# Down projection of a gated feed-forward layer: one token tile's second product moved to the end and split in two column pieces

## Chip, cores, metric

The kernel runs on one core of a Trainium2 chip. The metric is device time of one execution in microseconds (us), lower is better. The median before was 273.38 us (3 runs, 273.16 to 274.22). Five things work side by side on the core: the tensor engine (PE; PEld is its weight loading), the vector engine (DVE), the scalar engine (ACT), GpSimd (POOL), and the queues that start DMAs (here mostly SP's). Data lies in the on-chip memory SBUF; PE writes its sums to PSUM, used here as eight banks.

## The reference

```python
def reference(x, w_gate, w_up, w_down):          # x 32x32x1024, F = 3584, all bf16
    return (_gelu(x @ w_gate) * (x @ w_up)) @ w_down
```

So there are 1024 tokens; the last step, the down projection, multiplies a 1024x3584 matrix by a 3584x1024 one. The change touches only this step.

## The kernel before

The down projection is one level of a Strassen scheme: the operands are seen as 2x2 blocks, and seven block products are made in the order 1, 2, 7, 5, 6, 3, 4. Products 1 and 2 multiply the bf16 data directly; the operands of the others are held as f32r (fp32r in the profile), for 7, 5 and 6 sums or differences made by DVE. Each product is 4 token tiles of 128 rows times 14 steps of 128 (NK = 14), each step a matmul of 512 columns. A PSUM bank holds one tile. Product 1 is used twice: product 2 is added to it to give an output block (the sum goes out from `o11`), and a copy of it in the banks PB is where product 6 is added.

```python
        PA, PB = (0, 1, 2, 3), (4, 5, 6, 7)
        F, H = 0.2266, 0.216                      # planned us of one matmul, f32r and bf16
        begin = {}
        now = base
        for n in (1, 2, 7, 5, 6, 3, 4):
            begin[n] = now
            now += 4 * NK * (H if n < 3 else F)
        end = now
        EDGE = 4

        def sweep(n, banks, start, stat, mov, done, prep=None):
            steps = [(t, k) for k in range(EDGE) for t in range(3)] + [(3, k) for k in range(EDGE)]
            steps += [(t, k) for k in range(EDGE, NK - EDGE) for t in range(4)]
            steps += [(t, k) for t in range(4) for k in range(NK - EDGE, NK)]
            if n < 3:
                steps = [(t, k) for t in range(4) for k in range(NK)]
            # ... [cut: for every step one matmul; after a tile's last step, done(t, planned time)]

        sweep(1, PA, True, lambda k, t: ht(0, 0, k, t), lambda k: wd[0][0][:, k, :],
              lambda t, at: act(bank(PB[t]), bank(PA[t]), COPY, at))

        def done2(t, at):
            act(o11[:, t, :], bank(PA[t]), COPY, at)
            out_dma(0, t, 0, o11[:, t, :])
        sweep(2, PA, False, lambda k, t: ht(0, 1, k, t), lambda k: wd[1][0][:, k, :], done2)
        # ... [cut: prep7, prep5, prep6, prep3, prep4: DVE and ACT make the operands of the other products]
        def done4(t, at):
            if t % 2 == 0:
                pr.add("dve", "tensor_copy", late[:, 2, t, :], bank(PA[t]), at=at)
            else:
                act(late[:, 2, t, :], bank(PA[t]), COPY, at)
            out_dma(1, t, 0, late[:, 2, t, :])
        # ... [cut: sweeps 7, 5, 6, 3]
        sweep(4, PA, False, lambda k, t: S[:, c_at(1, k), t * P:(t + 1) * P], one_w(2), done4, prep4)
```

Every instruction goes through a small recorder that finds the dependences itself, in SBUF by cells of 256 bytes and in PSUM by whole banks. And on every engine but PE the instructions are put in the order of a planned time `at`, so the order is fixed before the kernel runs.

```python
    GRAIN = 256
    def cells(self, ap):
        # ... [cut]
        found.update(range(s // self.GRAIN, (s + run - 1) // self.GRAIN + 1))
    def finish(self, nc, es):
        for e in self.ENGINES:
            if e != "pe":
                self.ops[e].sort(key=lambda op: (op.at, op.index))
```

## Time and profile before

| quantity | value | from |
|---|---|---|
| time, median of 3 runs | 273.38 us | timed runs |
| span of the profiled execution | 976.1 us | the page |
| start of one 512-column matmul to the next | 0.84 us | timeline |
| ACT copy of 128x512 / DVE copy of 128x512 | 0.597 / 0.692 us | instruction groups by shape |
| store of 128 KB, issue to landing | 1.7 us | DMA issues |
| end of the last matmul to the end of the span | 2.76 us | trace: 976.13 - 973.37 |

The page of the kernel before, its head, its chain that ended last and the costliest group (columns of a group: busy us, mean ns of one, then idle time before):

```profile
span 976.1 us, 3280 instructions
PE 966.8 (99%) x1182; PEld 436.0 (45%) x1192; DVE 208.5 (21%) x237; ACT 134.8 (14%) x210; POOL 36.6 (4%) x23
...
PE 99%; issue 1%; ACT 0%
...
L117 PE MATMUL ps<-S,T 128*128 128x512 f32 x560 | 465.4, 1102 | 0.0
```

PE bounds the kernel. But this execution is 3.6 times as long as the timed ones: matmuls started 0.84 us apart. Its records give a granted clock of 1.00 all the same, so what slowed it is not shown. The end of its timeline (columns: start us, length us, engine, instruction, count, idle time before and its releaser):

```profile
959.09 14.28 PE L117 MATMUL ps<-T,S 128*128 128x512 f32 x17
...
966.84 0.60 ACT L117 ACTIVATE arena<-ps 128x512 bf16<-128x512 f32 x1 [12.01 <-PE ps L117]
...
973.40 0.60 ACT L117 ACTIVATE arena<-ps 128x512 bf16<-128x512 f32 x1 [5.97 <-PE ps L117]
```

17 matmuls in 14.28 us are 0.84 us each. The last thing PE releases is an ACT copy of 0.60 us; then only the store of 128 KB remains.

### The profile page before, as it was taken

Reading aid. Unit: us, or ns where it says so; the run is one execution under the profiler, and the core shown is the slowest. Engines: PE = TensorE matmul, PEld = TensorE weight load, DVE = VectorE, ACT = ScalarE, POOL = GpSimd, SP = SyncE. Lnnn points to the kernel's source line nnn. Section 1 sums busy time; section 2 is a strip of 40 time slices with the busy share of each in tenths; the row PEclk is TensorE's granted clock in tenths of the full one; section 3 lists DMA queues with packets and bytes.
Section 4 is the critical chain, followed back from the end, with each engine's and each line's share of the span. In section 5 each row is a group of like instructions: output and inputs, shape, how many; then the busy total and the mean of one; then the engine's idle time right before and its main releaser. Section 6 shows DMA issues by size and latency. Waiting matters only on the chain.

```text
span 976.1 us, 3280 instructions
## 1 busy us (share of the span) xinstructions
PE 966.8 (99%) x1182; PEld 436.0 (45%) x1192; DVE 208.5 (21%) x237; ACT 134.8 (14%) x210; POOL 36.6 (4%) x23
## 2 busy tenths in 40 slices
PE   9999999999999999999999999999999999999998
PEld 3222235555555555555444443442224555555554
DVE  0112222123212321231120202045000433114100
ACT  0011122111221112121111120100000000012110
POOL 0000000000000000001101010000000000000000
DMA  5530100101301003003000020400000000000000
GB/s 129 134 82 0 43 0 1 43 0 37 92 1 43 0 0 119 0 2 85 1 0 0 2 74 0 150 1 1 0 11 11 1 0 0 0 0 22 16 5 21
DMA packets 46895, 27.46 MB, mean 28 GB/s; under 512 B 8480, under 2 KB 46880, under 8 KB 46880
## 3 DMA queue, kind: packets, MB, share of 16 engines
q1 hardware_dynamic: 44656, 25.30, 9.4%
q10 hardware_dynamic: 2224, 1.97, 0.8%
q8 instruction: 9, 0.15, 0.1%
q14 instruction: 6, 0.05, 0.0%
HBM read 23.33 MB, written 2.10 MB: 26 GB/s over the span
## 4 chain that ended last, share of the span: by engine, by line
PE 99%; issue 1%; ACT 0%
PE ps L117 99%; ACT arena L117 0%
## 5 line engine op out<-in xcount | busy, mean ns | idle before, releaser
L117 PE MATMUL ps<-S,T 128*128 128x512 f32 x560 | 465.4, 1102 | 0.0
L117 PEld LDWEIGHTS ps<-S,T 128*128 128x128 f32 x560 | 240.2, 429 | 221.0 <-issue 212.7
L117 PE MATMUL ps<-T,S 128*128 128x512 f32 x224 | 185.2, 1098 | 0.0
L117 PE MATMUL ps<-arena 128*128 128x512 bf16 x186 | 155.2, 1105 | 3.4 <-issue 3.4
L117 PEld LDWEIGHTS ps<-T,S 128*128 128x128 f32 x224 | 96.0, 429 | 88.1 <-issue 88.1
L117 PEld LDWEIGHTS ps<-arena 128*128 128x128 bf16 x192 | 41.4, 221 | 113.9 <-issue 108.7
L117 PE MATMUL ps<-arena,hT 128*128 128x512 bf16 x109 | 90.2, 1106 | 1.9 <-issue 1.9
L117 ACT ACTIVATE tmp<-ps 128x512 f32<-128x512 f32 x64 | 38.1, 597 | 335.3 <-PE ps L117 335.3
L117 DVE TENSOR_TENSOR hT<-tmp,ps 128x512 bf16<-128x512 f32 x56 | 38.5, 687 | 189.9 <-PE ps L117 187.5
L117 DVE TENSOR_TENSOR tmp<-ps,tmp 128x512 f32<-128x512 f32 x28 | 19.4, 692 | 244.4 <-PE ps L117 244.4
L117 ACT ACTIVATE ps<-ps 128x512 f32<-128x512 f32 x44 | 25.6, 582 | 233.7 <-PE ps L117 233.7
L117 DVE TENSOR_TENSOR T<-arena,T 128x1024 fp32r<-128x1024 bf16 x42 | 51.0, 1220 | 29.9 <-PE ps L117 29.8
L117 POOL TENSOR_TENSOR T<-arena 128x1024 fp32r<-128x1024 bf16 x17 | 35.9, 2123 | 528.4 <-DVE T L117 499.5
L117 PEld LDWEIGHTS ps<-arena,hT 128*128 128x128 bf16 x112 | 24.5, 221 | 67.1 <-issue 66.5
L117 DVE TENSOR_TENSOR T<-arena 128x1024 fp32r<-128x1024 bf16 x25 | 30.0, 1219 | 104.6 <-PE ps L117 104.6
L117 PE MATMUL ps<-S 128*128 128x512 f32 x56 | 46.3, 1092 | 0.0
L117 PEld LDWEIGHTS ps<-S 128*128 128x128 f32 x56 | 23.9, 427 | 22.0 <-issue 22.0
L117 DVE TENSOR_TENSOR ps<-ps,tmp 128x512 f32<-128x512 f32 x32 | 22.3, 698 | 53.0 <-PE ps L117 53.0
L117 ACT ACTIVATE tmp<-tmp 128x512 f32<-128x512 f32 x28 | 17.7, 631 | 67.7 <-DVE tmp L117 67.7
L117 PE MATMUL ps<-arena,tmp 128*128 128x512 bf16 x31 | 26.1, 1100 | 0.5 <-issue 0.5
L117 ACT ACTIVATE hT<-ps 128x512 f32<-128x512 f32 x14 | 8.4, 597 | 67.8 <-PE ps L117 67.8
L117 DVE TENSOR_TENSOR S<-hT,S 128x1024 fp32r<-128x1024 bf16 x7 | 8.6, 1226 | 39.0 <-PE ps L117 39.0
(29 smaller groups left out, 112.6 us busy)
## 6 DMA issues: line engine op xcount, KB each, us to landing
arena<-in_w_down_dram SPq DMA_DIRECT2D x4, 1792.0 KB, 9.4
arena<-in_w_gate_dram SPq DMA_DIRECT2D x10, 512.0 KB, 4.1
arena<-in_w_up_dram SPq DMA_DIRECT2D x10, 512.0 KB, 5.4
out_dram<-arena SPq DMA_DIRECT2D x12, 128.0 KB, 1.7
arena<-in_w_gate_dram SPq DMA_DIRECT2D x4, 256.0 KB, 5.0
arena<-in_w_up_dram SPq DMA_DIRECT2D x4, 256.0 KB, 5.0
arena<-in_w_up_dram ACTq DMA_DIRECT2D x4, 128.0 KB, 4.7
arena<-in_w_gate_dram ACTq DMA_DIRECT2D x2, 256.0 KB, 2.8
```

What stands on the lines that cost most here:

```text
L117: ins = name(eng, *args, **kw) if callable(name) else getattr(eng, name)(*args, **kw)
```

## The change

Intent: what follows the last matmul (copy, issue, store) is paid in full, so let the last piece of work be small. One tile of product 2 waits until everything else is done. It is split at column 384, into two banks; the first piece is copied by ACT and stored while PE still works on the second. As product 1's copy in PB is used up by product 6, tile 3 of product 1 is kept in an SBUF tile `p1` meanwhile. A sweep begins with three of its tiles and holds the fourth back for a while, so that ACT has time to empty that tile's bank; which tile is held back changes in product 7. The diff, cut to its core:

```diff
+        p1 = sb("p1", [P, 512], FP32)
         for n in (1, 2, 7, 5, 6, 3, 4):
             begin[n] = now
-            now += 4 * NK * (H if n < 3 else F)
-        end = now
+            now += (3 if n == 2 else 4) * NK * (H if n < 3 else F)
+        end = now + NK * H
 # ... [cut] in sweep: product 7 holds back tile 2, the others tile 3; product 2 has 3 tiles
+            held = 2 if n == 7 else 3
+            steps = [(t, k) for k in range(EDGE) for t in range(4) if t != held] + [(held, k) for k in range(EDGE)]
             if n < 3:
-                steps = [(t, k) for t in range(4) for k in range(NK)]
+                steps = [(t, k) for t in range(5 - n) for k in range(NK)]
 # ... [cut]
+        def done1(t, at):
+            act(bank(PB[t]), bank(PA[t]), COPY, at)
+            if t == 3:
+                act(p1[:, :], bank(PA[t]), COPY, at)
 # ... [cut] after sweep 4:
+        pieces = ((PB[0], 0, 384), (PB[1], 384, 512))
+        for b, c0, c1 in pieces:
+            act(ps[:, b, 0:c1 - c0], p1[:, c0:c1], COPY, begin[4] + 6)
+        for b, c0, c1 in pieces:
+            for k in range(NK):
+                mm(b, ht(0, 1, k, 3), wd[1][0][:, k, c0:c1], False, k == NK - 1, add=True)
+            if c0 == 0:
+                act(o11[:, 3, c0:c1], ps[:, b, 0:c1 - c0], COPY, end)
+            else:
+                pr.add("dve", "tensor_copy", o11[:, 3, c0:c1], ps[:, b, 0:c1 - c0], at=end)
+            dma("sp", out_r[:, 3, c0:c1], o11[:, 3, c0:c1], end, "out")
```

## The prediction

> **What bounds the kernel now.** The tensor engine: the page gives PE busy for 99% of the span, DVE 21%, ACT 14%, and 99.0% of the chain that ended last is matmuls. The profiled execution took 976.1 us though the timed runs took 273.38: its matmuls start every 0.84 us (17 in 14.28 us, timeline of the end), while 1182 matmuls in 273 us leave at most 0.23 us each. Its "granted clock 1.00" can't be right. The Trainium skill, "TensorE: Matmul & The Clock Gate", Part 1, warns that clock events are unreliable and that the gate has been seen stuck at one quarter; 0.84 us agrees with that (its warm 215.7 ns for 512 columns, times 3.9). So I use the profile for ACT, DVE and DMA durations and for order, not for PE durations or waits.
>
> **What the change does.** The fourth token tile's second product (14 matmuls of 512 columns, bf16) leaves the second sweep and comes last, as 14 of 384 and 14 of 128 columns. Added: one ACT copy of the first product to SBUF, and two back into free PSUM banks (0.60, then an estimated 0.48 and 0.25 us, from 0.597 us for 128x512), where ACT is mostly idle: off the path. The later sweeps begin 14 x 0.216 = 3.02 us (the program's own slot length) earlier. DVE prepares their operands at 1.22 us a piece. By the program's schedule the seventh product's are ready 5.6 us before it begins, 2.6 after the change. For the fifth and sixth, the earlier PE also frees their slots earlier, so DVE's waits move along. The tile held back in the seventh product becomes the third, whose bank is now released last: 12 matmuls still cover the 0.6 us copy. I expect no new PE stall.
>
> **Cost on the path: PE.** The columns are the same, but 14 more weight loads and matmuls come. With the skill page's warm rate (N/2.4 + 2.5 ns), 14 x 162.5 + 14 x 55.8 = 3.06 us against 3.02; at the page's sustained 81 ns per 128-column matmul, 3.41. The slow trace has 128-column transposes every 0.21 us, a quarter of 0.84, so there the load hides. Cost 0.04 to 0.4 us, estimate 0.2.
>
> **Gain on the path: the tail.** Before, the last matmul's end (973.38) is followed by a 0.60 us ACT copy, a 0.33 us DMA issue and the landing (1.7 us); the span ends at 976.1: 2.7 us. After, a DVE copy of 128x128 ends it, estimated at 0.29 us (128x512 took 0.692, 128x256 of bf16 0.292). The 384-column copy runs on ACT during the last 14 matmuls. The last DMA carries 32 KB instead of 128, in 256-byte rows; its time is mostly fixed: 0 to 0.2 us. Gain 0.3 to 0.5 us.
>
> **Net.** 0.1 to 0.3 us faster, on 273.38, whose own runs spread over 1.06. Predicted 273.15 us, 272.4 to 273.9. Faster by over 2%: 0.01; within 2%: 0.98; slower by over 2%: 0.01.
>
> **What would show the steps.** 1196 matmuls; no gap at the starts of the seventh, fifth, sixth product; a DVE copy of about 0.29 us after the last matmul instead of 0.60 on ACT; landing of the last DMA 1.5 to 1.7 us; last matmul to span end about 2.3 instead of 2.7 us; the last 28 matmuls within 3.5 us at full clock (four times that at a quarter).
>
> **What would make it wrong.** A DVE-bound stretch at full clock, hidden in the slow profile, so that the earlier sweeps meet unready operands (up to +3 us); slow small stores; weight loads that 128-column matmuls don't hide (over 0.4 us).

## The result, and the profile after

273.11 us median (272.7 to 273.49, 6 runs) against 273.44 for the kernel before in the same rounds (273.04 to 274.22, 6 runs). Ratio 0.9985, 95% interval 0.9968 to 1.0003. A ratio here is the mean time of one kernel's fast runs over that of the other's of the same rounds, so it isn't quite the ratio of the medians quoted. The change is the same as before by the 2% measure, inside the predicted 272.4 to 273.9.

The profile after was taken at full clock. To have something to lay it beside, the kernel before was run once more as an experiment (run 1 below), and its profile is at full clock too. Head and end of the chain (start us, length us, what), kernel before at full clock:

```profile
span 271.0 us, 3290 instructions
PE 267.2 (99%) x1192; PEld 190.4 (70%) x1192; DVE 203.2 (75%) x237; ACT 131.9 (49%) x210; POOL 37.1 (14%) x23
...
268.27 0.02 issue
268.29 0.60 ACT arena L117
```

After the change:

```profile
span 271.2 us, 3314 instructions
PE 267.6 (99%) x1197; PEld 191.8 (71%) x1206; DVE 203.5 (75%) x238; ACT 132.8 (49%) x213; POOL 37.2 (14%) x23
...
269.01 0.02 issue
269.04 0.29 DVE o L117
```

DVE is really 75% busy, not 21%. The last link of the chain went from 0.60 us on ACT to 0.29 us on DVE. (1206 matmuls are in the program after and 1192 before, by the weight loads; some PE records are missing.) The spans alone, 271.0 and 271.2, would say that the change cost 0.2 us. They can't be compared like that: the code ahead of the down projection is the same in both, yet the down projection's first bf16 weight load starts at different times. Weight loads around that point, before and after:

```profile
180.41 1.62 PEld L117 LDWEIGHTS ps<-arena,hT 128*128 128x128 bf16 x9 [0.26 <-issue]
```

```profile
181.12 0.98 PEld L117 LDWEIGHTS ps<-arena,hT 128*128 128x128 bf16 x6 [0.26 <-issue]
```

That is 0.70 us apart. Over 13 profiles it lies between 180.41 and 181.47 us, a scatter of 1.06 us that comes from the part that nobody changed. So I measure from this weight load ("the anchor") to the end of the span, and split that at the end of the last matmul (which the profile models; the sum doesn't depend on it):

| us | before (run 1) | after |
|---|---|---|
| anchor to end of last matmul | 87.84 | 87.88 |
| end of last matmul to end of span ("tail") | 2.76 | 2.20 |
| anchor to end of span | 90.60 | 90.09 |

The change takes 0.52 us off: +0.04 on PE, -0.56 in the tail (worked out before rounding, here and below, so a last digit can differ by one). The tail in the two timelines. Before, at full clock:

```profile
267.87 0.39 PE L117 MATMUL ps<-T,S 128*128 128x512 f32 x1
268.11 1.14 SPq L117 DMA_DIRECT2D out_dram<-arena  x2
268.29 0.60 ACT L117 ACTIVATE arena<-ps 128x512 bf16<-128x512 f32 x1 [1.22 <-PE ps L117]
```

After (PE's line has one matmul of 384 columns and the 14 of 128):

```profile
267.89 1.11 PE L117 MATMUL ps<-arena,hT 128*128 128x384 bf16 x15
...
268.25 0.49 ACT L117 ACTIVATE o<-ps 128x384 bf16<-128x384 f32 x1 [1.69 <-PE ps L117]
268.77 0.92 SPq L117 DMA_DIRECT2D out_dram<-o  x2
269.04 0.29 DVE L117 CAST o<-ps 128x128 bf16<-128x128 f32 x1 [3.29 <-PE ps L117]
```

ACT's copy of the wide piece and the issue of its store are over (about 269.10) before DVE's copy ends (269.33), so nothing but the narrow piece remains. The DMA issues of after (count, size, median us from issue to landing) say what that is worth at the landing:

```profile
out_dram<-o SPq DMA_DIRECT2D x3, 128.0 KB, 1.7
out_dram<-o SPq DMA_DIRECT2D x1, 96.0 KB, 1.6
out_dram<-o SPq DMA_DIRECT2D x1, 32.0 KB, 1.4
```

Of the 0.56 us, 0.31 is the copy (0.60 - 0.29), and the remaining 0.25 is the smaller store. The copy also went from ACT to DVE, but that isn't what makes it shorter: in run 4 below ACT copies 128x128 in 0.28 us, and 128x512 takes DVE 0.69. The Trainium skill, "DMA: Bandwidth & Descriptors", section "Anatomy of one DMA", fits a DMA as a fixed time plus bytes / 436e9 seconds. For 98,304 bytes fewer that is an estimate of 0.225 us, and the trace comes within 0.03 us of it; its fixed 2.0 us (given for the path by way of GpSimd) is more than the 1.4 us measured here in all.

### The profile page after: what moved, and what is told of

Same layout as the page of the kernel before. It is cut to its first block, busy times and chain, and to the rows that moved or that the text cites. A ratio compares the mean times of both kernels' runs of the same rounds, so it can differ in the third digit from the quotient of the medians.

```text
span 271.2 us, 3314 instructions
## 1 busy us (share of the span) xinstructions
PE 267.6 (99%) x1197; PEld 191.8 (71%) x1206; DVE 203.5 (75%) x238; ACT 132.8 (49%) x213; POOL 37.2 (14%) x23
## 4 chain that ended last, share of the span: by engine, by line
PE 99%; issue 0%; DVE 0%
PE ps L117 99%; DVE o L117 0%
## 5 line engine op out<-in xcount | busy, mean ns | idle before, releaser
L117 PE MATMUL ps<-S,T 128*128 128x512 f32 x560 | 129.2, 391 | 0.0
L117 PEld LDWEIGHTS ps<-S,T 128*128 128x128 f32 x560 | 105.1, 188 | 22.5
L117 PE MATMUL ps<-T,S 128*128 128x512 f32 x224 | 51.3, 390 | 0.0
L117 PEld LDWEIGHTS ps<-T,S 128*128 128x128 f32 x224 | 42.0, 188 | 8.8
L117 PE MATMUL ps<-arena 128*128 128x512 bf16 x186 | 42.6, 384 | 0.4
L117 PEld LDWEIGHTS ps<-arena 128*128 128x128 bf16 x192 | 17.8, 98 | 24.3 <-issue 3.2
L117 PE MATMUL ps<-arena,hT 128*128 128x512 bf16 (+2 forms) x124 | 24.3, 355 | 0.1
L117 DVE TENSOR_TENSOR S<-hT 128x1024 fp32r<-128x1024 bf16 x14 | 16.6, 1219 | 0.0
L117 ACT ACTIVATE T<-arena 128x1024 fp32r<-128x1024 bf16 x14 | 14.8, 1059 | 0.0
L117 PE MATMUL ps<-S 128*128 128x512 f32 x56 | 12.9, 389 | 0.0
```

What stands on the lines that cost most here:

```text
L117: ins = name(eng, *args, **kw) if callable(name) else getattr(eng, name)(*args, **kw)
```

## The experiments

Twelve runs were made; three of them repeat the kernel before or the change. My theory after the result: moving the product is free, cutting it is almost free in bf16, and the gain is the shorter tail. Rivals: the old order held a stall at full clock which the new one removes; or the earlier start of the later products brings the gain. All twelve and the change, in the anchored measure and in time:

| run | PE, anchor to last matmul's end | tail | sum | ratio to before, 95% interval |
|---|---|---|---|---|
| 1 e1_before_again | 87.84 | 2.76 | 90.60 | 0.9987 [0.9967, 1.0006] |
| 12 e12_before_third | 87.84 | 2.76 | 90.61 | 0.9991 [0.9975, 1.0008] |
| the change | 87.88 | 2.20 | 90.09 | 0.9985 [0.9968, 1.0003] |
| 5 e8_after_again | 87.88 | 2.20 | 90.08 | 0.9977 [0.9959, 0.9994] |
| 2 e2_move_uncut | 87.85 | 2.76 | 90.61 | 1.0012 [0.9992, 1.0033] |
| 7 e3_cut_in_place | 88.20 | 2.77 | 90.97 | 1.0017 [0.9998, 1.0036] |
| 3 e4_cut_last_f32 | 88.75 | 2.51 | 91.25 | 1.0012 [0.9992, 1.0031] |
| 4 e6_wide_last | 87.88 | 2.65 | 90.53 | 1.0006 [0.9985, 1.0026] |
| 8 e7_cut_448_64 | 87.88 | 4.05 | 91.94 | 1.0051 [1.0031, 1.0071] |
| 9 e9_cut_448_64_apart | 87.88 | 2.50 | 90.39 | 0.9998 [0.9981, 1.0014] |
| 10 e10_cut_480_32_apart | 88.00 | 2.59 | 90.59 | 0.9997 [0.9979, 1.0014] |
| 6 e5_move_four | 97.07 | 2.20 | 99.28 | 1.0300 [1.0281, 1.0319] |
| 11 e11_move_two | 87.92 | 2.20 | 90.12 | 0.9983 [0.9963, 1.0002] |

### 1 and 12: the kernel before against itself

Edit: none.

> The kernel before, run against itself, for its noise and for a profile at full clock. Ratio 1.000 within 0.002. Theory (the change is worth only its tail): in the trace, product starts are 216 ns (bf16) and 227 ns (f32r) apart to the end with no gap over 0.1 us where the seventh, fifth and sixth products start, the last matmul is followed by an ACT copy of 0.60 us, and from the end of the last matmul to the end of the span it is about 2.6 us against 2.2 after the change. Rival (the old order held a stall at full clock that the new order removes): a gap of 0.2 us or more on the tensor engine somewhere in the down projection, absent in the trace of after.

> The kernel before against itself once more, for a second trace at full clock and the noise. Theory: 90.60 us within 0.05 from the down projection's start to the end, tail 2.76 us; ratio 1.000 within 0.002. Rival (the first trace was off): a value nearer to 90.1.

Measured: 273.64 us against 273.86 and 273.65 against 273.94. Timed against itself the kernel comes out at 0.9987 and 0.9991, so timed runs can't tell the change's 0.9985 from nothing. The anchored sums repeat within 0.01 us (90.60 and 90.61), so the trace can. In the down projection of both traces every gap between matmul starts over 0.24 us is either two spacings (a missing record) or stands where product 7 begins, where two starts are 28 and 418 ns apart, together again two spacings; the trace of after has the same pair there. There is none where products 5 and 6 begin: the stall of the rival didn't exist.

### 5: the change again

Edit: none.

> The change again, for a second trace. From the first matmul of the down projection to the end of the span its first trace has 90.08 us and the kernel before, run against itself, has 90.60. Theory (a fixed tail gain of about 0.5 us): 90.1 within 0.05 again. Rival (one lucky trace): anywhere between 90.1 and 90.6. In the timed runs, whose A/A ratio was 0.9987 +- 0.002, I expect a ratio of about 0.998, not resolved.

Measured: 272.93 us against 273.44, sum 90.08: the gain of 0.52 us repeats. The timed interval lies below 1 this time, which with the first result and the two self-comparisons is still too near the noise to rest on.

### 2: moved, not cut

```diff
-        pieces = ((PB[0], 0, 384), (PB[1], 384, 512))
+        pieces = ((PB[0], 0, 512),)
```

> The tile's second product comes last as in the change, but in one piece of 512 columns with one ACT copy and one store of 128 KB. Theory (moving is free, the gain is the cut tail): as the kernel before, ratio 1.000 within 0.001, last matmul to span end about 2.6 us. Rival (the earlier start of the later products gives the gain): as fast as the change, ratio 0.9985.

Measured: 274.32 us against 273.86; sum 90.61, tail 2.76. As in the kernel before, to 0.01 us. The move alone brings and costs nothing; the rival of the earlier start falls.

### 7: cut, not moved, eight times over

```diff
# in the kernel before, products 1 and 2, all tiles; both pieces in the same bank
+                if n < 3:
+                    if k == 0:
+                        for c0, c1 in ((0, 384), (384, 512)):
+                            for kk in range(NK):
+                                pr.add("pe", "matmul", ps[:, banks[t], c0:c1], stat(kk, t), mov(kk)[:, c0:c1],
+                                       start=start and kk == 0, stop=kk == NK - 1, skip_group_check=True)
+                else:
-                mm(banks[t], stat(k, t), mov(k), start and k == 0, k == NK - 1, add=not start)
+                    mm(banks[t], stat(k, t), mov(k), start and k == 0, k == NK - 1, add=not start)
```

> The kernel before in its old order; all eight tiles of the first and second product are computed as 384 and 128 columns in the same bank (112 more matmuls), copies and stores uncut. Measures the cutting cost alone, eight times over. Theory (the trace of after: 162.5 and 55.8 ns, together 2.3 ns over one of 512 columns): 112 x 2.5 ns = 0.28 us slower, ratio 1.001. Rival (81 ns for a 128-column matmul with its weight load, as the prediction allowed): 112 x 27 ns = 3.1 us slower, ratio 1.011.

Measured: 274.14 us against 273.44, PE 0.35 us longer than before. Divided by 112 that is 3.2 ns for each additional matmul. The starts are 162.5 and 55.8 ns apart, where an uncut one takes 215.8: that is 2.5 ns each, 0.28 us in all, and another 0.06 us is lost in the step from the last cut matmul to product 7. The skill page's 81 ns for a 128-column matmul, which my prediction left open, is out.

The result was wrong (relative error 0.31). The Trainium skill, "PSUM — Partial Sum Buffer", section "The four PSUM rules", says that a matmul which starts a group clears the written-marks of the whole bank, not only of its own columns. The second piece of product 1 would then clear those of the first, and product 2 would overwrite those columns instead of adding. That fits, but no run here isolates it. The instructions and the time are unaffected. In the change the pieces lie in two banks and never start a group, so it is correct.

### 3: cut where the kernel ended before, in f32r

```diff
# in sweep, in the kernel before; the store of tile 3 is cut in two likewise
+                if n == 4 and t == 3:
+                    if k == 0:
+                        act(ps[:, PB[0], 0:128], ps[:, PA[3], 384:512], COPY, begin[4] + 0.5)
+                    for b, c0, c1 in ((PA[3], 0, 384), (PB[0], 384, 512)) if k < NK - EDGE else ():
+                        mm(b, stat(k, t), mov(k)[:, c0:c1], False, False, add=True)
+                    if k == NK - 1:
+                        for b, c0, c1 in ((PA[3], 0, 384), (PB[0], 384, 512)):
+                            for kk in range(NK - EDGE, NK):
+                                mm(b, stat(kk, t), mov(kk)[:, c0:c1], False, kk == NK - 1, add=True)
```

> Order as in the kernel before; only its last tile (fourth product, f32r operands) is cut in columns 0 to 383 and 384 to 511, in two banks, copied and stored apart as in the change. Theory (f32r is why the bf16 product had to be moved): the trace of after shows weight loads of 188 ns for f32r and 98 ns for bf16, so a 128-column f32r matmul can't follow the next in 56 ns; I estimate 0.19 us for each, so 14 x (0.19 + 0.19 - 0.227) = +2.1 us of tensor engine, less 0.35 us of tail: 1.8 us slower than before, ratio about 1.006. Rival (the move was needless): 0.3 us faster than before, ratio 0.999.

Measured: 274.31 us against 273.86; sum 91.25, that is 0.65 us slower than before and 1.17 slower than the change. The direction was right and the size wrong: PE lost 0.90 us, not 2.1. In the trace a 384- and a 128-column f32r matmul start 174 and 61 ns before the next one, but the 512-column matmul after them then takes 281 ns instead of 227; four 128-column ones in a row stand 60, 109 and 113 ns apart. So the estimate of 0.19 us each from the length of the weight load record (188 ns) was wrong: that record isn't the pace. In bf16 the same cut costs 0.04 us for a whole tile. The tail gained only 0.25 us. In its last timeline ACT's copy of the wide piece ends at 269.97, after DVE's narrow copy has begun; the last four narrow matmuls are too short a cover, so the second store's issue comes right behind the first's (it starts at 270.37, 0.20 us after DVE is done at 270.17):

```profile
269.48 0.49 ACT L117 ACTIVATE arena<-ps 128x384 bf16<-128x384 f32 x1 [1.02 <-PE ps L117]
269.88 0.29 DVE L117 CAST arena<-ps 128x128 bf16<-128x128 f32 x1 [0.41 <-PE ps L117]
```

So cutting the old last tile, done this way, loses. The move, which by itself brings nothing, gives a bf16 product to cut and 14 narrow matmuls in a row to hide the wide piece behind.

### 4: the wide piece last

```diff
-        pieces = ((PB[0], 0, 384), (PB[1], 384, 512))
+        pieces = ((PB[0], 0, 128), (PB[1], 128, 512))
```

> The change with the pieces swapped: columns 0 to 127 first, 128 to 511 last (DVE copies 384 columns, 96 KB in the last store). Theory (the gain is mostly the shorter last copy): same tensor engine time, last copy about 0.56 us instead of 0.29, so 0.27 us slower than the change, ratio to before about 0.9995. Rival (the gain comes from cutting or moving as such): as the change, ratio 0.9985.

Measured: 274.09 us against 273.86; PE the same to 0.01 us, tail 2.65. That is 0.45 us worse than the change, not 0.27. The end of the timeline:

```profile
269.24 0.56 DVE L117 CAST o<-ps 128x384 bf16<-128x384 f32 x1 [3.29 <-PE ps L117]
269.82 0.33 SPq L117 DMA_DIRECT2D out_dram<-o  x1
```

The copy is the 0.27 us expected; the rest, 0.18, is the larger last store (96 KB instead of 32: 1.62 us to landing instead of 1.44), which the expectation had left out.

### 8 and 9: a cut at column 448, without and with a place of its own

```diff
# run 8
-        pieces = ((PB[0], 0, 384), (PB[1], 384, 512))
+        pieces = ((PB[0], 0, 448), (PB[1], 448, 512))
# run 9, besides
+        last = arena[:, 8192:8192 + 64]
-                pr.add("dve", "tensor_copy", o11[:, 3, c0:c1], ps[:, b, 0:c1 - c0], at=end)
-            dma("sp", out_r[:, 3, c0:c1], o11[:, 3, c0:c1], end, "out")
+                pr.add("dve", "tensor_copy", last, ps[:, b, 0:c1 - c0], at=end)
+            dma("sp", out_r[:, 3, c0:c1], o11[:, 3, c0:c1] if c0 == 0 else last, end, "out")
```

> The change with the cut at column 448, so the last piece is 64 columns (16 KB store). Theory (a tail of copy, issue and landing, each with a fixed part): last copy about 0.22 us instead of 0.29 (0.56 for 384 columns and 0.29 for 128 give 0.16 us + 1.04 ns a column), landing at most 0.1 us less, so a tail of 2.05 to 2.15 us instead of 2.20; but 14 matmuls of 64 columns with weight loads of 98 ns may start only every 35 to 50 ns, so the tensor engine gains or loses under 0.2 us. From the down projection's start to the end 90.0 to 90.2 us. Rival (weight loads bound the 64-column pieces at 98 ns each): 0.9 us more on the tensor engine, about 90.8 us.

Measured in run 8: 274.98 us against 273.44, tail 4.05 us. Neither theory had that. Its timeline names the cause:

```profile
269.04 2.37 SPq L117 DMA_DIRECT2D out_dram<-o  x2
270.83 0.23 DVE L117 CAST o<-ps 128x64 bf16<-128x64 f32 x1 [5.23 <-DMA out_dram<-o]
```

DVE's copy waits for a DMA, the store of the wide piece. Column 448 is at byte 896, in the middle of a 256-byte cell, so the recorder believes that the copy overwrites what the store still reads. At 384 (byte 768) the pieces don't share a cell. I formed a new theory, that this wait is the whole loss:

> The cut at column 448 again, but the last piece is copied to a place of its own, so that its copy doesn't wait for the store of the first piece. Theory (the 1.9 us lost with the cut at 448 were that wait alone, a false dependence: the program tracks SBUF in cells of 256 bytes, and column 448 is at byte 896, in the middle of one): no wait, tail about 2.1 us against 2.20 of the change, 89.9 to 90.05 us from the down projection's start to the end, ratio about 0.998. Rival (a 64-column copy or a store of 128-byte rows is slow by itself): a tail over 3 us, ratio 1.005.

Measured in run 9: 273.89 us against 273.94, tail 2.50. The wait is gone, and with it 1.55 us; but the tail is still 0.30 us longer than the change's, not 0.1 shorter. The rest is in the queue:

```profile
268.20 0.54 ACT L117 ACTIVATE o<-ps 128x448 bf16<-128x448 f32 x1 [2.07 <-PE ps L117]
268.61 0.23 DVE L117 CAST arena<-ps 128x64 bf16<-128x64 f32 x1 [3.29 <-PE ps L117]
268.77 0.33 SPq L117 DMA_DIRECT2D out_dram<-o  x1
269.15 0.43 SPq L117 DMA_DIRECT2D out_dram<-arena  x1
```

DVE is done at 268.84, but SP is still issuing the wide piece's store until 269.10, so the narrow one's starts at 269.15, 0.58 us after the last matmul's end (268.57). In the change it is 0.36 us (269.36 - 269.00). The wide piece needs its copy and its issue, 0.54 + 0.33 us, and 14 matmuls of 64 columns, 29.2 ns apart, cover only 0.41 us of that; 14 of 128 columns cover 0.78. The landing gained nothing either: 16 KB took 1.5 us here, the change's 32 KB 1.4. That isn't the size alone. In run 8 the same 16 KB, issued long after the store before it, landed in 1.4 us too (the last DMA issue of run 8, then of run 9):

```profile
out_dram<-o SPq DMA_DIRECT2D x1, 16.0 KB, 1.4
out_dram<-arena SPq DMA_DIRECT2D x1, 16.0 KB, 1.5
```

In all three runs where the last store's issue starts some 0.045 us after the end of the one before it (3, 9 and 10), it takes 0.43 to 0.45 us instead of 0.33, and the landing is about 0.1 us later. So crowding the queue seems to cost twice: the wait for it and a longer issue. (In these three the last piece also comes from `arena` instead of `o11`, but the other stores from `arena` mostly take 0.33 us.)

On PE the cuts at 384 and 448 cost the same, so the rival of run 8 (98 ns for each short matmul, the length of a weight load record) is out.

### 10: narrower still

```diff
-        last = arena[:, 8192:8192 + 64]
-        pieces = ((PB[0], 0, 448), (PB[1], 448, 512))
+        last = arena[:, 8192:8192 + 32]
+        pieces = ((PB[0], 0, 480), (PB[1], 480, 512))
```

> As the run with 448 and 64, cut at 480: the last piece has 32 columns. Theory (every part of the tail has a fixed share, and short matmuls meet a floor): 14 x 202.5 ns + 14 x 25 to 29 ns = 3.19 to 3.24 us of tensor engine against 3.06 with 64 columns, copy 0.19 us instead of 0.22: 0.05 to 0.15 us worse than the cut at 448, about 90.1 us. Rival (the narrower the better): below 89.9 us.

Measured: 273.7 us against 273.94; sum 90.59, PE 0.12 us more than with 64 columns, just under the 0.13 to 0.18 expected (starts 25 ns apart, where the formula N/2.4 + 2.5 would give 15.8), tail 2.59. It loses 0.20 us to the cut at 448 and nearly all of the gain over before. The narrow store (8 KB) landed in 1.5 us, no faster than the 16 KB of run 9, which was issued as close behind another. The expectation had left out the queue: the last store's issue starts 0.67 us after the last matmul's end, 0.09 later than in run 9.

### 6: four tiles moved

```diff
-            now += (3 if n == 2 else 4) * NK * (H if n < 3 else F)
+            now += (0 if n == 2 else 4) * NK * (H if n < 3 else F)
-        sweep(2, PA, False, lambda k, t: ht(0, 1, k, t), lambda k: wd[1][0][:, k, :], done2)
+        p1 = arena[:, 8192:12288].bitcast(FP32).rearrange("p (t n) -> p t n", n=512)
+        for t in range(4):                       # product 1 is saved from PB during product 5
+            act(p1[:, t, :], bank(PB[t]), COPY, begin[5] + 9 + 0.1 * t)
-        pieces = ((PB[0], 0, 384), (PB[1], 384, 512))
+        pieces = [(t, PB[t], 0, 512) for t in range(3)] + [(3, PB[3], 0, 384), (3, PA[0], 384, 512)]
```

The edit also drops the held tile 2 and adapts the loops of copies. Why move so many? My prediction said that DVE's waits move along with PE, so that an earlier start is free. At full clock the trace lets one see how far. The operands that DVE makes go to a few places (slots) in turn, so DVE has to wait until PE has used what lies in a slot. DVE around that wait, before and after:

```profile
199.46 1.23 DVE L117 TENSOR_TENSOR S<-hT 128x1024 fp32r<-128x1024 bf16 x1
208.07 1.23 DVE L117 TENSOR_TENSOR T<-arena 128x1024 fp32r<-128x1024 bf16 x1 [7.38 <-PE ps L117]
```

```profile
200.17 1.22 DVE L117 TENSOR_TENSOR S<-hT 128x1024 fp32r<-128x1024 bf16 x1
205.74 1.23 DVE L117 TENSOR_TENSOR T<-arena 128x1024 fp32r<-128x1024 bf16 x1 [4.35 <-PE ps L117]
```

Starting the later products 3.03 us earlier ate 3.03 us of this wait. 4.35 us are left, and from there on DVE works without a wait up to product 6's last operand.

> All four tiles of the second product come last (the last one cut as in the change); the seventh product begins 9.1 us earlier than in the change. Theory: moving is free only while DVE waits for slots: in the trace of after it waits 4.35 us at 201.4 us and then works without a wait until the sixth product's last operand at 234.2 us. With four moved it can't restart before 201.4, so that operand comes at about 229.8 us of the same clock while the sixth product wants it at about 228.2: one stall of 1.6 us in the sixth product; about 91.7 us from the down projection's start to the end, 1.1 us slower than before (ratio 1.004), 1.6 slower than the change. Rival (DVE's waits always move along, as the prediction argued): no stall, 90.1 us, ratio 0.998.

Measured: 281.75 us against 273.44, 3.0% slower. PE's waits in its timeline (idle before, releaser):

```profile
192.51 35.30 PE L117 MATMUL ps<-T,S 128*128 128x512 f32 x154
229.31 3.47 PE L117 MATMUL ps<-T,S 128*128 128x512 f32 x14 [1.51 <-DVE T L117]
232.62 1.52 PE L117 MATMUL ps<-S 128*128 128x512 f32 x6
238.55 14.29 PE L117 MATMUL ps<-S 128*128 128x512 f32 x50 [4.41 <-DVE S L117]
```

The first stall is the one worked out beforehand: measured as excess between matmul starts it is 1.79 us, against 1.6. But there is a second one that I had not foreseen, 4.57 us in product 3. DVE's line shows why: coming late, it meets eight sums of the finished products which the fixed order has put before product 3's second operand.

```profile
229.17 1.22 DVE L117 TENSOR_TENSOR S<-hT,S 128x1024 fp32r<-128x1024 bf16 x1
230.69 0.70 DVE L117 TENSOR_TENSOR ps<-ps,tmp 128x512 f32<-128x512 f32 x1 [0.30 <-ACT ps L117]
...
236.15 1.22 DVE L117 TENSOR_TENSOR T<-arena,T 128x1024 fp32r<-128x1024 bf16 x1
237.28 2.35 DVE L117 TENSOR_TENSOR S<-hT,S 128x1024 fp32r<-128x1024 bf16 x2
```

The planned times of the sums count from the product starts, which moved; those of the operands count from the beginning of the down projection, which didn't. In the trace of after the operands still come first. And after these 4.41 us of idling PE starts some 12 matmuls only every 427 ns, where the records give a granted clock of 0.50; with the edges that costs another 2.78 us. The Trainium skill, "TensorE: Matmul & The Clock Gate", Part 1, gives 426.7 ns as the spacing of 512-column matmuls at half clock, and says that some 3.4 us of idling bring the half clock back; this trace agrees: the half clock follows the 4.41 us, and not the 1.51 us of the first stall. The three sum to 9.14 of the 9.19 us by which the anchored sum exceeds the change's. The second stall belongs to this program's unretuned order; so the run shows that moving isn't free without bound, not what four well-ordered moved tiles would cost.

### 11: two tiles moved

As run 6, with two tiles (2 and 3) moved and tile 1 held back in product 7:

```diff
-            now += (3 if n == 2 else 4) * NK * (H if n < 3 else F)
+            now += (2 if n == 2 else 4) * NK * (H if n < 3 else F)
-        pieces = ((PB[0], 0, 384), (PB[1], 384, 512))
+        pieces = [(2, PB[0], 0, 512), (3, PB[1], 0, 384), (3, PB[2], 384, 512)]
```

> Two tiles of the second product come last, the last one cut at 384. Theory (a tile may be moved for nothing as long as DVE still waits for a slot: the 4.35 us that it waits in the trace of after leave room for one more tile of 3.02 us): a wait of about 1.3 us left on DVE, no stall on the tensor engine, 90.1 us from the down projection's start to the end, ratio 0.998. Rival (every tile moved costs: a quarter to a third of what four cost): 1.5 to 2.7 us slower, ratio 1.005 to 1.010.

Measured: 273.22 us against 273.94; sum 90.12, 0.04 us from the change. DVE's wait is down to what the theory said, 1.3 us:

```profile
202.22 1.23 DVE L117 TENSOR_TENSOR T<-arena 128x1024 fp32r<-128x1024 bf16 x1 [1.36 <-PE ps L117]
```

So moving is free as long as this wait lasts, and not by the tile. There is no gain in a second tile either (90.12 against 90.09): only the last one has a tail.

No run beat the change. What the timelines of runs 9 and 10 suggest, issuing the two last stores from different queues, was not tried; nor was any cut between 128 and 384 or between 384 and 448.

## Why the prediction was right

- **Time.** Predicted 273.15 us (272.4 to 273.9), measured 273.11. That hit proves little: the range also holds the 273.44 of the kernel before, so no effect at all would have fallen in it, and how close 273.15 came is luck. Predicted 0.1 to 0.3 us faster. The medians of the same rounds say 0.33, the anchored traces 0.52, twice over, which is outside that. The timed runs alone don't distinguish this from nothing; what the traces confirm is the mechanism.
- **PE bounds the kernel; the slow profile's durations of ACT, DVE and DMA can be used.** Right: at full clock PE has 99%, the 128x512 copies take 0.60 and 0.69 us as in the slow trace, and the 128x128 copy the 0.29 estimated from it. The 1196 matmuls forecast were 1206: the slow trace lacks 10 records.
- **Moving costs no stall, DVE's waits move along.** Right for one tile (run 2 to 0.01 us) and for two (run 11), and wrong for four (run 6): the argument holds only while DVE waits for slots. The schedule's 5.6 and 2.6 us ahead of product 7 are 7.1 and 4.1 in the traces (from the end of the last of its DVE operands to its first matmul); the difference of 3.0 is right.
- **PE cost "0.04 to 0.4 us, estimate 0.2".** It is 0.04, the low end. The narrow matmuls start 55.8 ns apart, so the page's formula N/2.4 + 2.5 ns held to a tenth of a nanosecond, while the page's 81 ns would have cost 3.1 us in run 7, which showed 0.35.
- **Tail "0.3 to 0.5 us".** It is 0.56. The copy is as predicted (0.29 after 0.60). The mis-sized term is the store: "its time is mostly fixed: 0 to 0.2 us" measured 0.25 (its landing took 1.44 us, not 1.5 to 1.7), and run 4, with 96 KB last, showed 0.18 of it directly.
- **Both slips go the same way**, so the net was 0.52 instead of the stated 0.1 to 0.3. The difference is 0.1% of the kernel's time, which is why the range still held it.

## What to carry to other kernels

When one engine is busy all the time and its work stays as it is, what is left to gain lies after its last instruction: make the last piece small, but long enough on the engine that the copy and the issue of the piece before it are hidden behind it (here 0.78 us of matmuls for a 0.49 us copy and a 0.33 us issue; with 0.41 us the gain was more than halved). Choose the operand type that cuts cheaply, and keep the pieces apart in the units of whatever tracks dependences. To see half a microsecond in a kernel whose start scatters by one, measure in the trace from a fixed instruction just ahead of the changed code, and run the unchanged kernel against itself.

## What the Trainium skill lacked or had wrong

- "TensorE: Matmul & The Clock Gate", section "Back-to-back issue gap", gives about 81 ns (128 columns) and 131 ns (512) as the sustained spacing of matmuls that each load weights. Here, each with its own load, it was 55.8 and 215.8 ns (run 7), and 29.2 ns at 64 columns (run 9). The N/2.4 + 2.5 that this section calls isolated is what a stream shows here, as Part 1 of the same page has it; its floor of about 25 ns appeared at 32 columns (run 10).
- I found no page that gives matmul spacing for f32r. Measured: 226.6 ns at 512 columns; 384 and 128 columns alternating with longer ones 174 and 61 ns, with the next 512-column one stretched to 281; at 128 columns in a row 109 to 113 ns (run 3).
- The same page, section "LDWEIGHTS (loading the stationary operand)", has columns / 1.2, so 107 ns for 128. The records here last 98 ns (bf16) and 188 ns (f32r), and neither sets the pace: 64-column bf16 matmuls with a load each start every 29.2 ns (run 9), and 128-column f32r ones every 109 to 113 (run 3).
- "DMA: Bandwidth & Descriptors", section "Anatomy of one DMA": the part by bytes agrees (0.225 us estimated, 0.25 measured), but a store from the SP queue to HBM took 1.7 us (128 KB) and 1.4 us (32 KB in 256-byte rows) from issue to landing, less than the fixed 2.0 us given for the path by way of GpSimd; for the SP queue I found no time to landing. The time that the queue is busy with one issue (0.33 us here, 0.43 to 0.45 for the last stores of runs 3, 9 and 10, right behind another), which decided runs 9 and 10, isn't in that anatomy; the page has it only beside a trn3 feature, as cycles of earlier generations.
